# Re-interleaving all steps of a fused attention and highway kernel, with six short runs of dummy matmuls added

## The chip, the cores and the metric

The kernel runs on one core of a Trainium2 chip. The metric is the device time of one execution in microseconds (us). Eight executions of the kernel before were timed; their median is what the changed kernel is compared with. A traced execution adds, for every instruction of every engine, when it started and how long it was busy. The engines are TensorE (PE in the profile, with PEld for its weight loads), VectorE (DVE), ScalarE (ACT), GpSimd (POOL) and SyncE (SP), which here only issues DMAs.

## What is computed

`q`, `k`, `v` have shape 8 x 8 x 576 x 64 (batch, head, sequence, head size). An efficient attention is followed by a highway layer on 4608 tokens of width 512:

```python
q_s = softmax(q, over the 64 of a head)
k_s = softmax(k, over the 576 of the sequence)
kv  = einsum('bhsd,bhse->bhde', k_s, v)
x   = einsum('bhsd,bhde->bhse', q_s, kv)      # then (b, s) x (h, e): 4608 x 512
H   = max(x @ w_h, 0)
T   = sigmoid(x @ w_t + b_t)
out = T * H + (1 - T) * x
```

Inputs and output are float32; the matmuls run in float16.

## The kernel before, in words

The work is cut into batches b = 0 to 7, and into 37 kinds of step. Each kind is a small function, and one list, `order`, written out in the source, calls some 550 of them one after the other. Every engine executes its own share of that list strictly in the list's order, so the list decides all the queues; semaphores between engines are derived from the buffers.

For a batch, the steps are these.

- `load(b, "q" | "k" | "v")` issues one DMA of 1152 KB on SP's queue (two of 576 KB where a third argument 2 is given); `load_weight` brings `w_t` (one DMA of 1024 KB) and `w_h` (four of 256 KB). Each of the four input pools has three buffers; the weights pass through the same buffers as q and k. In the built program every DMA also waits until the DMA issued eight before it has completed.
- `exp_half` (ACT, L174) takes the exponential of half the heads of q or k. `cast_v` and `cast_v_head` bring v to float16 (POOL L185 and L193, ACT L191).
- `kv_half` (PE, 36 small matmuls, tile `psk`) forms k-transposed times v and, with a column of ones, the sums of k; `kv_norm` (DVE L212, L213) divides.
- `q_sums` or `q_sums_tree` (DVE L224, or L235 to L237), `q_recip` (DVE L242), then `q_scale_p` on POOL (L254; batch 0 has `q_scale_v` on DVE) normalise q. `q_trans` (PE, tile `pq`) and `q_copy` (DVE L274) transpose it; for batches 6 and 7 `q_turn` does that with two DMA transposes (L283, tile `qsD`) instead.
- `x_pair` and `x_left` (PE, tiles `px`, `px_l`) form x transposed; `x_copy` (ACT or DVE), `x_left_copy` and `x9_done` take it out of PSUM.
- The highway layer works in chunks c = 0 to 7, one per batch, and 8 and 9, which hold what 512 columns leave of each batch. For each chunk and each of four output blocks there is a `gate` (four matmuls, tile `pt`) with `tanh` on ACT (L392), a `carry` (four matmuls, tile `ph`) with `diff` on DVE (L405), and then `blend` on DVE (L413) and for some blocks `add_x` on POOL (L424). Here one `gate` or one `carry` of a chunk 0 to 7 is called a unit; there are 64.
- `out_tile` and `tile9` turn the result round on PE (tile `nat`), `out_copy` (L464) and `tile9_copy` copy it to a staging buffer and every fourth copy issues a 1 MB store. `last9` is the last of all.

The weights have steps of their own: `less_one` (POOL L122) subtracts the identity from `w_h`, and `cast_weight` casts one quarter of a matrix to float16, on POOL or DVE (L117) or ACT (L115). `gate_bias` turns the bias round on PE.

`warm_up(n)` issues n matmuls of a constant 128 x 512 operand whose result nobody reads, and `warm_mid(n, i, home)` does the same into a bank of its own. The kernel before issues 46 such dummies: 42 of them ahead of the first `q_trans`, two after `kv_norm(0)` in the list, two ahead of the first gate.

PSUM has four banks in the pool `ht`, two in `q2` and one each in `q1` and `nat`; a gate or a carry holds an `ht` bank from its first matmul until `blend` or `diff` has read it.

Of the kernel before, what the change touches and what calls it, by code (L numbers as in the profile page):

```python
# [18 lines left out]
def kernel(  # L19
# [12 lines left out]
    P = 128  # L32
# [422 lines left out]
    nat, nat2 = {}, {}  # L455
# [36 lines left out]
    def last9():  # L492
# [19 lines left out]
        ("warm_up", 24), ("load", 0, "q", 2), ("exp_half", 0, "q", 0), ("load", 1, "q"),  # L512
        ("load", 0, "v", 2), ("cast_v", 0, 1), ("warm_up", 6), ("exp_half", 0, "q", 1),
        ("warm_up", 1), ("q_sums", 0, 1), ("load", 0, "k", 2), ("warm_up", 4),
        ("warm_up", 2), ("load_bias",), ("cast_v", 0, 0), ("q_sums", 0, 0),
        ("load_weight", "t", "q32"), ("q_recip", 0), ("warm_mid", 5),
        ("q_scale_v", 0, 4, 9), ("q_trans", 0, 1, "q2"), ("exp_half", 1, "q", 0),
        ("load_weight", "h", "k32", 4), ("q_scale_v", 0, 0, 4), ("q_copy", 0, 1),
        ("load", 1, "k"), ("exp_half", 1, "q", 1), ("cast_weight", "t", 3, "P"),
        ("exp_half", 0, "k", 0), ("less_one", 1), ("q_trans", 0, 2, "nat"),  # L520
        ("q_sums_tree", 1, 0), ("q_sums_tree", 1, 1), ("q_trans", 0, 0),
        ("exp_half", 0, "k", 1), ("load", 1, "v", 2), ("kv_half", 0, 0), ("q_recip", 1),
        ("q_copy", 0, 2), ("kv_half", 0, 1), ("cast_weight", "t", 1, "P"), ("q_copy", 0, 0),
        ("kv_norm", 0), ("warm_up", 2), ("load", 2, "q"), ("less_one", 2),
        ("x_pair", 0, 0, False), ("cast_weight", "t", 0, "V"), ("less_one", 0),
        ("x_pair", 0, 1, False, ("ht", "ht")), ("x_copy", 0, 0, "AA"),
        ("x_copy", 0, 1, "AV"), ("gate_bias",), ("x_left", 0),
        ("cast_weight", "h", 1, "A", 0.5), ("less_one", 3), ("cast_weight", "t", 2, "V"),
        ("warm_up", 2), ("cast_weight", "h", 2, "A", 0.5),
        ("cast_weight", "h", 3, "A", 0.5), ("cast_weight", "h", 0, "A", 0.5),  # L530
        ("x_left_copy", 0), ("q_scale_p", 1, 4, 8), ("gate", 0, 2, "q2"), ("gate", 0, 0),
        ("gate", 0, 3, "nat"), ("tanh", 0, 2), ("exp_half", 1, "k", 1), ("carry", 0, 2),
        ("load", 2, "v", 2), ("q_trans", 1, 1), ("carry", 0, 1), ("diff", 0, 2),
        ("q_scale_p", 1, 0, 4), ("q_copy", 1, 1), ("tanh", 0, 0),
        ("cast_v_head", 1, 2, "P"), ("cast_v_head", 1, 1, "P"), ("exp_half", 1, "k", 0),
        ("cast_v_head", 1, 3, "A"), ("carry", 0, 0), ("blend", 0, 2), ("q_trans", 1, 0),
        ("gate", 0, 1), ("cast_v_head", 1, 0, "A"), ("kv_half", 1, 1), ("load", 2, "k"),
        ("diff", 0, 1), ("diff", 0, 0), ("tanh", 0, 1), ("q_copy", 1, 0), ("kv_half", 1, 0),
        ("blend", 0, 0), ("kv_norm", 1), ("q_scale_p", 1, 8, 9), ("q_trans", 1, 2),
        ("x_pair", 1, 0, False, ("ht", "ht")), ("tanh", 0, 3), ("exp_half", 2, "q", 0),  # L540
        ("q_copy", 1, 2), ("blend", 0, 1), ("x_pair", 1, 1, False, ("ht", "q2")),
        ("cast_v_head", 2, 2, "P"), ("x_copy", 1, 0, "AV"), ("x_copy", 1, 1, "AV"),
        ("gate", 1, 1), ("exp_half", 2, "q", 1), ("add_x", 0, 0), ("carry", 1, 2),
        ("cast_v_head", 2, 3, "A"), ("tanh", 1, 1), ("load", 3, "q"), ("q_sums_tree", 2, 0),
        ("cast_v_head", 2, 0, "P"), ("q_sums_tree", 2, 1), ("carry", 1, 1), ("diff", 1, 1),
        ("x_left", 1), ("carry", 0, 3), ("load", 3, "v"), ("gate", 1, 0),
        ("cast_v_head", 2, 1, "A"), ("q_recip", 2), ("exp_half", 2, "k", 1), ("tanh", 1, 0),
        ("load", 3, "k"), ("diff", 0, 3), ("blend", 1, 1), ("q_scale_p", 2, 0, 4),
        ("x_left_copy", 1), ("q_scale_p", 2, 8, 9), ("carry", 1, 0), ("q_scale_p", 2, 4, 8),
        ("diff", 1, 2), ("exp_half", 2, "k", 0), ("q_trans", 2, 0, "q1"),  # L550
        ("exp_half", 3, "q", 0), ("exp_half", 3, "q", 1), ("kv_half", 2, 1), ("diff", 1, 0),
        ("q_copy", 2, 0), ("load", 4, "q"), ("kv_half", 2, 0), ("gate", 1, 2),
        ("cast_v", 3, 1), ("blend", 0, 3), ("q_trans", 2, 1, "q1"), ("kv_norm", 2, 0, 1),
        ("blend", 1, 0), ("q_copy", 2, 1), ("carry", 1, 3),
        ("x_pair", 2, 0, False, ("nat", "q1")), ("add_x", 1, 1), ("kv_norm", 2, 1, 2),
        ("tanh", 1, 2), ("load", 4, "k"), ("q_trans", 2, 2, "q2"), ("load", 5, "q"),
        ("blend", 1, 2), ("x_copy", 2, 0, "AA"), ("q_sums", 3, 0), ("diff", 1, 3),
        ("gate", 1, 3), ("load", 4, "v"), ("x_pair", 2, 1, False, ("nat", "q1")),
        ("tanh", 1, 3), ("x_copy", 2, 1, "AV"), ("gate", 2, 1), ("cast_v", 3, 0),
        ("q_sums", 3, 1), ("carry", 2, 0), ("q_copy", 2, 2), ("exp_half", 3, "k", 1),  # L560
        ("q_recip", 3), ("gate", 2, 2), ("exp_half", 3, "k", 0), ("exp_half", 4, "q", 0),
        ("add_x", 1, 0), ("add_x", 0, 1), ("x_left", 2), ("blend", 1, 3),
        ("out_tile", 0, 1), ("q_scale_p", 3, 0, 4), ("exp_half", 4, "q", 1),
        ("x_left_copy", 2), ("diff", 2, 0), ("q_sums", 4, 0), ("carry", 2, 3),
        ("kv_half", 3, 0), ("diff", 2, 3), ("out_copy", 0, 1, "A"), ("exp_half", 4, "k", 1),
        ("kv_half", 3, 1), ("tanh", 2, 1), ("load", 5, "k"), ("q_scale_p", 3, 4, 9),
        ("q_trans", 3, 0, "q1"), ("carry", 2, 1), ("out_tile", 0, 0), ("q_copy", 3, 0),
        ("q_trans", 3, 1, "q1"), ("kv_norm", 3), ("out_copy", 0, 0, "A"),
        ("q_trans", 3, 2, "q2"), ("load", 6, "q"), ("diff", 2, 1), ("tanh", 2, 2),
        ("gate", 2, 0), ("exp_half", 5, "q", 1), ("q_copy", 3, 2), ("q_copy", 3, 1),  # L570
        ("q_sums", 4, 1), ("q_recip", 4), ("x_pair", 3, 0, True), ("out_tile", 0, 2),
        ("carry", 2, 2), ("x_copy", 3, 0, "A"), ("x_pair", 3, 1, True),
        ("out_copy", 0, 2, "A"), ("out_tile", 0, 3), ("q_scale_p", 4, 0, 4),
        ("blend", 2, 1), ("diff", 2, 2), ("x9_done", 3), ("tanh", 2, 0), ("blend", 2, 0),
        ("load", 5, "v"), ("gate", 2, 3), ("q_trans", 4, 0, "q1"), ("blend", 2, 2),
        ("q_sums", 5, 1), ("x_copy", 3, 1, "A"), ("q_copy", 4, 0), ("q_scale_p", 4, 4, 9),
        ("load", 7, "v"), ("carry", 3, 1), ("gate", 3, 0), ("load", 7, "q"),
        ("exp_half", 5, "q", 0), ("cast_v", 4, 0), ("carry", 3, 0), ("out_copy", 0, 3, "A"),
        ("tanh", 2, 3), ("q_trans", 4, 1, "q1"), ("out_tile", 0, 4), ("cast_v", 4, 1),
        ("diff", 3, 1), ("exp_half", 4, "k", 0), ("carry", 3, 3), ("diff", 3, 0),  # L580
        ("out_copy", 0, 4, "A"), ("out_tile", 0, 5), ("q_copy", 4, 1),
        ("q_trans", 4, 2, "q1"), ("kv_half", 4, 0), ("q_sums", 5, 0), ("tanh", 3, 0),
        ("add_x", 2, 0), ("kv_half", 4, 1), ("q_copy", 4, 2), ("q_recip", 5),
# [105 lines left out]
```

## Time and profile before

| what | value |
|---|---|
| median of 8 executions | 127.03 us (126.52 to 127.65) |
| the profiled execution's own time | 127.47 us |
| its span, first to last instruction | 125.7 us |
| mean granted TensorE clock | 0.972 |
| busy: PE, PEld | 111.1 us, 60.9 us |
| busy: DVE, ACT, POOL | 94.6 us, 92.7 us, 78.7 us |
| DMA | 41.24 MB, mean 328 GB/s |
| read from HBM, written to it | 30.41 MB, 9.44 MB |

The page cuts the span into 40 slices of 3.14 us and gives each engine's busy share in tenths; the row PEclk is the clock that TensorE was granted, in tenths of full speed. Matmuls overlap in their pipeline, so PE busy is not PE at its peak. The chain of waits follows the work back from the last instruction. "Idle before" is what an engine waited for. Times of stretches can be asked for with the busy time of every engine and the clock.

### The profile page before, as it was taken

The page shows a single profiled execution, that of the slowest core. Times are in us where ns is not written, and L with a number is a line of the kernel's source. Part 1 is how long each engine was busy: PE and PEld are TensorE (multiplying, and loading weights), DVE is VectorE, ACT ScalarE, POOL GpSimd, SP SyncE. Part 2 cuts the span into 40 slices and gives each one's busy share as a digit, 9 for nine tenths or more (in the row PEclk, how much of TensorE's full clock was granted, in tenths as well). Part 3 has the DMA queues.
Part 4 walks back from the last instruction along what each step waited for, and adds up shares of the span by engine and source line. Part 5 has one row for each costly group of instructions (what it writes and reads, how often), then busy time and mean ns, then how long its engine had stood idle before and what let it go on. Part 6 is the DMA issues. An engine that isn't in the chain of part 4 may idle for free.

```text
span 125.7 us, 3329 instructions
## 1 busy us (share of the span) xinstructions
PE 111.1 (88%) x1359; PEld 60.9 (48%) x1359; DVE 94.6 (75%) x179; ACT 92.7 (74%) x130; POOL 78.7 (63%) x75
## 2 busy tenths in 40 slices
PE   4999637999597898999999999999998999999950
PEld 1344412345342632644574564555464545599840
DVE  1077696019999999999999999689774736799960
ACT  4427436892995969989969969999993966866760
POOL 2000712974355995935988999999999424864610
PEclk9999996579999999999999999999999999999999
DMA  3999999999999999999999999994782702409984
GB/s 114 351 364 403 408 408 403 412 411 411 414 405 411 413 398 411 411 410 405 412 406 417 414 410 412 416 245 91 284 192 50 334 0 125 209 5 415 409 347 169
DMA packets 20583, 41.24 MB, mean 328 GB/s; under 512 B 5460, under 2 KB 5976, under 8 KB 19544
## 3 DMA queue, kind: packets, MB, share of 16 engines
q1 hardware_dynamic: 20568, 41.03, 85.9%
q8 instruction: 10, 0.16, 0.5%
q14 instruction: 5, 0.04, 0.1%
HBM read 30.41 MB, written 9.44 MB: 317 GB/s over the span
## 4 chain that ended last, share of the span: by engine, by line
PE 35%; DMA 23%; DVE 18%; POOL 11%; issue 4%; ACT 4%; SPq 3%; DVEq 1%; POOLq 0%; ACTq 0%
PE pt L64 14%; PE ph L64 11%; DMA v<-in_v_dram 9%; DMA k<-in_k_dram 9%; POOL eq L254 8%; PE nat L64 4%; DVE dd L405 4%; DMA qsD<-eq 4%; DVE r L224 3%; SPq L94 3%; DVE g L413 2%; PE pq L69 2%; DVE qsT L274 2%; POOL v L185 1%; DVE xT L361 1%
## 5 line engine op out<-in xcount | busy, mean ns | idle before, releaser
L64 PE MATMUL pt<-xT,w16t 128*128 128x512 f16 x128 | 34.6, 401 | 1.9 <-DVE xT L361 1.0
L254 POOL TENSOR_TENSOR eq<-eq,r 128x1024 f16<-128x1024 f16 (+2 forms) x16 | 29.7, 1877 | 8.7 <-DVE r L242 7.7
L64 PE MATMUL ph<-xT,w16h 128*128 128x512 f16 x128 | 32.1, 379 | 0.0
L405 DVE SCALAR_TENSOR_TENSOR dd<-xT,ph 128x512 f16<-128x512 f16 x32 | 21.3, 680 | 12.8 <-PE ph L64 12.5
L424 POOL TENSOR_TENSOR g<-g,xT 128x512 f16<-128x512 f16 x23 | 26.1, 1155 | 6.4 <-DVE g L413 6.4
L392 ACT ACTIVATE pt<-pt,bt 128x512 f32<-128x512 f32 (+1 forms) x40 | 24.6, 627 | 6.2 <-PE pt L64 5.5
L413 DVE SCALAR_TENSOR_TENSOR g<-pt,dd 128x512 f16<-128x512 f32 (+1 forms) x40 | 24.5, 626 | 4.1 <-ACT pt L392 3.3
L174 ACT ACTIVATE eq<-q 128x1152 f16<-128x1152 f32 x16 | 18.4, 1168 | 6.6 <-DMA q<-in_q_dram 5.5
L64 PEld LDWEIGHTS <-w16t 128*128 128x128 f16 x160 | 15.1, 101 | 16.1 <-issue 5.1
L464 ACT COPY o<-nat 128x512 f32<-128x512 f32 x28 | 16.7, 599 | 7.5 <-PE nat L64 6.4
L185 POOL CAST v<-v 128x1152 f16<-128x1152 f32 x12 | 13.6, 1148 | 11.3 <-DMA v<-in_v_dram 11.3
L64 PEld LDWEIGHTS <-w16h 128*128 128x128 f16 x160 | 14.6, 98 | 12.4 <-issue 1.0
L174 ACT ACTIVATE ek<-k 128x1152 f16<-128x1152 f32 x16 | 18.8, 1182 | 2.4 <-DMA k<-in_k_dram 2.4
L224 DVE TENSOR_REDUCE r<-eq 128x18 f32<-128x1152 f16 x12 | 16.0, 1344 | 5.3 <-ACT eq L174 5.3
L64 PE MATMUL nat<-ident,g 128*128 128x128 f16 x142 | 14.6, 220 | 0.0
L64 PEld LDWEIGHTS <-g 128*128 128x128 f16 x144 | 11.3, 98 | 5.4 <-DVE g L413 0.9
L64 PE MATMUL warm<-wide,ident 128*128 128x512 f16 x41 | 11.9, 452 | 1.8 <-DVE wide L144 1.8
L274 DVE COPY qsT<-pq 128x1024 f16<-128x1024 f16 (+1 forms) x18 | 9.7, 547 | 1.8 <-PE pq L69 1.6
L357 ACT CAST xT<-px 128x1024 f16<-128x1024 f32 x10 | 10.2, 1025 | 0.5 <-PE px L64 0.5
L69 PE MATMUL pq<-ident,eq 128*128 128x128 f16 x108 | 8.6, 220 | 0.9 <-POOL eq L254 0.7
L64 PEld LDWEIGHTS <-ident 128*128 128x128 f16 x46 | 4.8, 109 | 8.2 <-issue 3.1
L69 PEld LDWEIGHTS <-eq 128*128 128x128 f16 x108 | 6.6, 98 | 4.3 <-POOL eq L254 2.5
(53 smaller groups left out, 101.6 us busy)
## 6 DMA issues: line engine op xcount, KB each, us to landing
out_dram<-o SPq DMA_DIRECT2D x8, 1024.0 KB, 4.5
q<-in_q_dram SPq DMA_DIRECT2D x7, 1152.0 KB, 14.4
k<-in_k_dram SPq DMA_DIRECT2D x7, 1152.0 KB, 14.4
v<-in_v_dram SPq DMA_DIRECT2D x5, 1152.0 KB, 14.5
v<-in_v_dram SPq DMA_DIRECT2D x6, 576.0 KB, 10.7
q<-in_q_dram SPq DMA_DIRECT2D x2, 576.0 KB, 4.2
k<-in_k_dram SPq DMA_DIRECT2D x2, 576.0 KB, 11.2
w32t<-in_moe_w_t_dram SPq DMA_DIRECT2D x1, 1024.0 KB, 12.5
```

Of the source, the lines that this page charges most:

```text
L64: mm = lambda o, l, r, st, sp: nc.tensor.matmul(o, l, r, start=st, stop=sp, skip_group_check=True)
L69: nc.tensor.matmul(o, i, ident, is_transpose=True, start=True, stop=True, skip_group_check=True,)
L174: nc.scalar.activation(dst[b][:, :, 2 * a : 2 * a + 2, :], in32[which][b][:, 2 * a : 2 * a + 2].rearrange("p c n d -> p n c d"), AF.Exp,)
L185: nc.gpsimd.tensor_copy(o, i)
L224: nc.vector.reduce_sum(qsum[b][:, :, h], eq[b][:, :, h, :], axis=AX.X)
L254: nc.gpsimd.tensor_mul(e, e, r.broadcast_to(list(e.shape)))
L274: nc.vector.tensor_copy(qsT[b][:, :, n0:n1, :], turned_q.pop((b, g)))
L392: nc.scalar.activation(ps, ps, AF.Tanh, bias=bt2[:, ob : ob + 1], scale=0.5)
L405: nc.vector.scalar_tensor_tensor(dd, xv(ob), -0.5, ps, op0=ALU.mult, op1=ALU.max)
L413: nc.vector.scalar_tensor_tensor(gv(ob), th, 1.0, dd, op0=ALU.add, op1=ALU.mult)
L424: eng.tensor_add(gv(ob), gv(ob), xv(ob))
L464: copy(rows_of_four((g, n // 4))[:, n % 4, :], nat.pop((g, n)))
```

## The change

Only the list `order` is changed; all functions are the same. It has the same real steps as before. Their order differs almost everywhere, on every engine. What can be told apart:

- The DMAs at the start go q0, k0, bias, q1, v0, w_h, w_t instead of q0, q1, v0, k0, bias, w_t, w_h; from batch 3 on q4 is ahead of v3 and k3, and v7 is issued after the two transposes of batch 6.
- Steps on the weights of `w_h` come ahead of those on `w_t`.
- `warm_mid(2, i, "ht")` appears six times (i = 10, 16, 11, 1, 7, 18); together with the existing runs, now placed differently, there are 58 dummies, 31 of them ahead of the first `q_trans` and 23 between it and the first gate.
- The two transposes of batch 7 change places.

The list up to chunk 2's first matmuls, and the places further down that the text below speaks of:

```diff
-        ("warm_up", 24), ("load", 0, "q", 2), ("exp_half", 0, "q", 0), ("load", 1, "q"),
-        ("load", 0, "v", 2), ("cast_v", 0, 1), ("warm_up", 6), ("exp_half", 0, "q", 1),
-        ("warm_up", 1), ("q_sums", 0, 1), ("load", 0, "k", 2), ("warm_up", 4),
-        ("warm_up", 2), ("load_bias",), ("cast_v", 0, 0), ("q_sums", 0, 0),
-        ("load_weight", "t", "q32"), ("q_recip", 0), ("warm_mid", 5),
-        ("q_scale_v", 0, 4, 9), ("q_trans", 0, 1, "q2"), ("exp_half", 1, "q", 0),
-        ("load_weight", "h", "k32", 4), ("q_scale_v", 0, 0, 4), ("q_copy", 0, 1),
-        ("load", 1, "k"), ("exp_half", 1, "q", 1), ("cast_weight", "t", 3, "P"),
-        ("exp_half", 0, "k", 0), ("less_one", 1), ("q_trans", 0, 2, "nat"),
-        ("q_sums_tree", 1, 0), ("q_sums_tree", 1, 1), ("q_trans", 0, 0),
-        ("exp_half", 0, "k", 1), ("load", 1, "v", 2), ("kv_half", 0, 0), ("q_recip", 1),
-        ("q_copy", 0, 2), ("kv_half", 0, 1), ("cast_weight", "t", 1, "P"), ("q_copy", 0, 0),
-        ("kv_norm", 0), ("warm_up", 2), ("load", 2, "q"), ("less_one", 2),
-        ("x_pair", 0, 0, False), ("cast_weight", "t", 0, "V"), ("less_one", 0),
-        ("x_pair", 0, 1, False, ("ht", "ht")), ("x_copy", 0, 0, "AA"),
-        ("x_copy", 0, 1, "AV"), ("gate_bias",), ("x_left", 0),
-        ("cast_weight", "h", 1, "A", 0.5), ("less_one", 3), ("cast_weight", "t", 2, "V"),
-        ("warm_up", 2), ("cast_weight", "h", 2, "A", 0.5),
-        ("cast_weight", "h", 3, "A", 0.5), ("cast_weight", "h", 0, "A", 0.5),
-        ("x_left_copy", 0), ("q_scale_p", 1, 4, 8), ("gate", 0, 2, "q2"), ("gate", 0, 0),
-        ("gate", 0, 3, "nat"), ("tanh", 0, 2), ("exp_half", 1, "k", 1), ("carry", 0, 2),
-        ("load", 2, "v", 2), ("q_trans", 1, 1), ("carry", 0, 1), ("diff", 0, 2),
-        ("q_scale_p", 1, 0, 4), ("q_copy", 1, 1), ("tanh", 0, 0),
-        ("cast_v_head", 1, 2, "P"), ("cast_v_head", 1, 1, "P"), ("exp_half", 1, "k", 0),
-        ("cast_v_head", 1, 3, "A"), ("carry", 0, 0), ("blend", 0, 2), ("q_trans", 1, 0),
-        ("gate", 0, 1), ("cast_v_head", 1, 0, "A"), ("kv_half", 1, 1), ("load", 2, "k"),
-        ("diff", 0, 1), ("diff", 0, 0), ("tanh", 0, 1), ("q_copy", 1, 0), ("kv_half", 1, 0),
-        ("blend", 0, 0), ("kv_norm", 1), ("q_scale_p", 1, 8, 9), ("q_trans", 1, 2),
-        ("x_pair", 1, 0, False, ("ht", "ht")), ("tanh", 0, 3), ("exp_half", 2, "q", 0),
-        ("q_copy", 1, 2), ("blend", 0, 1), ("x_pair", 1, 1, False, ("ht", "q2")),
-        ("cast_v_head", 2, 2, "P"), ("x_copy", 1, 0, "AV"), ("x_copy", 1, 1, "AV"),
-        ("gate", 1, 1), ("exp_half", 2, "q", 1), ("add_x", 0, 0), ("carry", 1, 2),
-        ("cast_v_head", 2, 3, "A"), ("tanh", 1, 1), ("load", 3, "q"), ("q_sums_tree", 2, 0),
-        ("cast_v_head", 2, 0, "P"), ("q_sums_tree", 2, 1), ("carry", 1, 1), ("diff", 1, 1),
-        ("x_left", 1), ("carry", 0, 3), ("load", 3, "v"), ("gate", 1, 0),
-        ("cast_v_head", 2, 1, "A"), ("q_recip", 2), ("exp_half", 2, "k", 1), ("tanh", 1, 0),
-        ("load", 3, "k"), ("diff", 0, 3), ("blend", 1, 1), ("q_scale_p", 2, 0, 4),
-        ("x_left_copy", 1), ("q_scale_p", 2, 8, 9), ("carry", 1, 0), ("q_scale_p", 2, 4, 8),
-        ("diff", 1, 2), ("exp_half", 2, "k", 0), ("q_trans", 2, 0, "q1"),
-        ("exp_half", 3, "q", 0), ("exp_half", 3, "q", 1), ("kv_half", 2, 1), ("diff", 1, 0),
-        ("q_copy", 2, 0), ("load", 4, "q"), ("kv_half", 2, 0), ("gate", 1, 2),
-        ("cast_v", 3, 1), ("blend", 0, 3), ("q_trans", 2, 1, "q1"), ("kv_norm", 2, 0, 1),
-        ("blend", 1, 0), ("q_copy", 2, 1), ("carry", 1, 3),
-        ("x_pair", 2, 0, False, ("nat", "q1")), ("add_x", 1, 1), ("kv_norm", 2, 1, 2),
...
-        ("load", 7, "v"), ("carry", 3, 1), ("gate", 3, 0), ("load", 7, "q"),
...
-        ("carry", 5, 3), ("q_turn", 6, 4, 9), ("x9_done", 5), ("exp_half", 6, "k", 1),
...
-        ("q_turn", 6, 0, 4), ("q_scale_p", 7, 0, 4), ("tanh", 5, 2), ("kv_norm", 6),
...
-        ("tanh", 5, 1), ("q_scale_p", 7, 4, 9), ("q_turn", 7, 0, 4), ("out_tile", 1, 4),
...
-        ("out_copy", 1, 4, "A"), ("q_turn", 7, 4, 9), ("x9_done", 6), ("add_x", 5, 2),
...
-        ("tile9", 0, 4), ("add_x", 9, 0), ("tile9_copy", 0, 4, "A"),
-        ("tile9_copy", 1, 4, "V"), ("carry", 9, 3), ("blend", 9, 2), ("gate", 9, 3),
-        ("tile9", 3, 3), ("tanh", 9, 3), ("diff", 9, 3), ("tile9", 2, 3),
-        ("tile9_copy", 2, 3, "A"), ("tile9_copy", 3, 3, "V"), ("blend", 9, 3), ("last9",),
+        ("load", 0, "q", 2), ("warm_mid", 2, 10, "ht"), ("load", 0, "k", 2),
+        ("exp_half", 0, "q", 1), ("load_bias",), ("warm_up", 24), ("load", 1, "q"),
+        ("load", 0, "v", 2), ("cast_v", 0, 0), ("load_weight", "h", "k32", 4),
+        ("cast_v", 0, 1), ("load_weight", "t", "q32"), ("exp_half", 0, "q", 0),
+        ("q_sums", 0, 1), ("q_sums", 0, 0), ("exp_half", 0, "k", 0),
+        ("exp_half", 0, "k", 1), ("exp_half", 1, "q", 0), ("warm_mid", 5), ("q_recip", 0),
+        ("q_scale_v", 0, 4, 9), ("q_trans", 0, 1, "q2"), ("q_scale_v", 0, 0, 4),
+        ("gate_bias",), ("q_copy", 0, 1), ("warm_up", 6), ("warm_up", 1), ("q_trans", 0, 0),
+        ("warm_up", 4), ("exp_half", 1, "q", 1), ("q_sums_tree", 1, 0), ("less_one", 0),
+        ("kv_half", 0, 0), ("q_sums_tree", 1, 1), ("warm_up", 2), ("q_recip", 1),
+        ("warm_mid", 2, 16, "ht"), ("less_one", 1), ("q_trans", 0, 2, "nat"),
+        ("kv_half", 0, 1), ("warm_mid", 2, 11, "ht"), ("load", 1, "k"), ("less_one", 2),
+        ("q_copy", 0, 0), ("load", 1, "v", 2), ("load", 2, "q"), ("q_scale_p", 1, 4, 8),
+        ("cast_weight", "h", 0, "A", 0.5), ("warm_mid", 2, 1, "ht"), ("kv_norm", 0),
+        ("cast_weight", "h", 2, "A", 0.5), ("x_pair", 0, 0, False), ("less_one", 3),
+        ("cast_weight", "t", 1, "P"), ("q_copy", 0, 2), ("cast_weight", "h", 1, "A", 0.5),
+        ("x_pair", 0, 1, False, ("ht", "ht")), ("x_copy", 0, 1, "AV"),
+        ("x_copy", 0, 0, "AA"), ("x_left", 0), ("cast_weight", "h", 3, "A", 0.5),
+        ("x_left_copy", 0), ("warm_up", 2), ("q_trans", 1, 1), ("cast_weight", "t", 3, "P"),
+        ("warm_up", 2), ("q_scale_p", 1, 0, 4), ("cast_weight", "t", 0, "V"),
+        ("cast_weight", "t", 2, "V"), ("gate", 0, 0), ("q_copy", 1, 1),
+        ("gate", 0, 2, "q2"), ("carry", 0, 2), ("q_trans", 1, 0), ("diff", 0, 2),
+        ("tanh", 0, 0), ("carry", 0, 0), ("cast_v_head", 1, 1, "P"), ("carry", 0, 1),
+        ("tanh", 0, 2), ("q_copy", 1, 0), ("cast_v_head", 1, 2, "P"), ("load", 2, "v", 2),
+        ("exp_half", 1, "k", 0), ("blend", 0, 2), ("exp_half", 1, "k", 1),
+        ("cast_v_head", 1, 0, "A"), ("gate", 0, 1), ("load", 2, "k"), ("diff", 0, 0),
+        ("kv_half", 1, 0), ("diff", 0, 1), ("cast_v_head", 1, 3, "A"),
+        ("q_scale_p", 1, 8, 9), ("tanh", 0, 1), ("cast_v_head", 2, 2, "P"),
+        ("exp_half", 2, "q", 0), ("blend", 0, 0), ("kv_half", 1, 1),
+        ("exp_half", 2, "q", 1), ("kv_norm", 1), ("q_trans", 1, 2),
+        ("x_pair", 1, 0, False, ("ht", "ht")), ("x_pair", 1, 1, False, ("ht", "q2")),
+        ("blend", 0, 1), ("x_copy", 1, 0, "AV"), ("x_copy", 1, 1, "AV"), ("carry", 0, 3),
+        ("q_copy", 1, 2), ("cast_v_head", 2, 0, "P"), ("load", 3, "q"),
+        ("gate", 0, 3, "nat"), ("tanh", 0, 3), ("x_left", 1), ("q_sums_tree", 2, 0),
+        ("cast_v_head", 2, 3, "A"), ("q_sums_tree", 2, 1), ("x_left_copy", 1),
+        ("q_recip", 2), ("q_scale_p", 2, 0, 4), ("gate", 1, 1), ("tanh", 1, 1),
+        ("carry", 1, 2), ("carry", 1, 1), ("exp_half", 2, "k", 0), ("diff", 0, 3),
+        ("diff", 1, 2), ("diff", 1, 1), ("blend", 0, 3), ("carry", 1, 0), ("blend", 1, 1),
+        ("diff", 1, 0), ("load", 4, "q"), ("gate", 1, 0), ("q_scale_p", 2, 4, 8),
+        ("cast_v_head", 2, 1, "A"), ("q_trans", 2, 0, "q1"), ("kv_half", 2, 0),
+        ("q_copy", 2, 0), ("exp_half", 2, "k", 1), ("gate", 1, 2), ("kv_norm", 2, 0, 1),
+        ("tanh", 1, 0), ("q_trans", 2, 1, "q1"), ("exp_half", 3, "q", 1), ("load", 3, "v"),
+        ("tanh", 1, 2), ("add_x", 0, 1), ("blend", 1, 0), ("q_scale_p", 2, 8, 9),
+        ("kv_half", 2, 1), ("q_copy", 2, 1), ("add_x", 1, 0), ("add_x", 1, 1),
+        ("kv_norm", 2, 1, 2), ("add_x", 0, 0), ("q_sums", 3, 1), ("gate", 1, 3),
+        ("exp_half", 3, "q", 0), ("q_sums", 3, 0), ("x_pair", 2, 0, False, ("nat", "q1")),
+        ("warm_mid", 2, 7, "ht"), ("load", 3, "k"), ("x_copy", 2, 0, "AA"),
...
+        ("gate", 4, 3), ("diff", 4, 2), ("q_turn", 6, 0, 4), ("out_tile", 1, 1),
+        ("x_copy", 5, 1, "A"), ("tanh", 4, 3), ("blend", 4, 2), ("add_x", 4, 0),
+        ("gate", 5, 2), ("q_turn", 6, 4, 9), ("carry", 5, 0), ("kv_half", 6, 1),
+        ("load", 7, "v"), ("out_copy", 1, 1, "A"), ("blend", 4, 1), ("add_x", 4, 2),
...
+        ("tanh", 5, 0), ("q_scale_p", 7, 0, 4), ("out_copy", 1, 3, "A"),
...
+        ("out_copy", 1, 5, "A"), ("blend", 5, 0), ("add_x", 5, 0), ("q_scale_p", 7, 4, 9),
+        ("carry", 5, 2), ("tanh", 5, 1), ("cast_v", 7, 1), ("x_pair", 6, 1, True),
+        ("cast_v", 7, 0), ("diff", 5, 1), ("diff", 5, 2), ("x_copy", 6, 1, "A"),
+        ("carry", 5, 3), ("q_turn", 7, 4, 9), ("out_tile", 1, 4), ("blend", 5, 2),
...
+        ("q_turn", 7, 0, 4), ("exp_half", 7, "k", 1), ("gate", 5, 3), ("carry", 6, 1),
...
+        ("carry", 9, 2), ("tile9", 1, 4), ("blend", 9, 1), ("tile9_copy", 0, 4, "A"),
+        ("gate", 9, 2), ("tanh", 9, 2), ("blend", 9, 0), ("gate", 9, 3), ("diff", 9, 2),
+        ("tile9_copy", 1, 4, "V"), ("blend", 9, 2), ("add_x", 9, 1), ("tanh", 9, 3),
+        ("blend", 9, 3), ("add_x", 9, 0), ("tile9", 3, 3), ("tile9", 2, 3),
+        ("tile9_copy", 2, 3, "A"), ("tile9_copy", 3, 3, "V"), ("last9",),
+        ("warm_mid", 2, 18, "ht"),
```

## The prediction

> **What bounds the kernel now.** I read the page's rows by slices first, then the chain of waits, then busy time by stretches of the first 27 us, then each engine's timeline there. The page:
>
> ```profile
> PE   4999637999597898999999999999998999999950
> DVE  1077696019999999999999999689774736799960
> POOL 2000712974355995935988999999999424864610
> PEclk9999996579999999999999999999999999999999
> DMA  3999999999999999999999999994782702409984
> ```
>
> From slice 15 (47 us) to slice 37, PE is nearly solid; DMA is full until 82 us, DVE from 28 us on. PE's holes and the only fall of the clock lie in the first third. So I add up PE's real work with the chain's prices where PE carries it: a unit 0.86 us (64: 55.3), the same for chunks 8 and 9 0.44 (16: 7.0), a batch's `kv_half` pair 0.73 (5.8), its three `q_trans` 1.01 (6.1), its x steps 0.80 (6.4), an `out_tile` 0.22 to 0.34 (9.0), `tile9` and `last9` 1.3. Sum: 90.9 us. From the first real matmul (12.98) to the last (121.7) pass 108.7, so 17.8 are lost. At `x_pair(1, 0)`, at 32.76, seven units, two kv pairs, six `q_trans` and one batch's x steps are done (10.3 us) in 19.8: 9.5 of the 17.8 go there, 8.3 in the next 89 us.
>
> Stretches of 3.4 us around that loss (columns: length, then busy of PE, PEld, DVE, ACT, POOL, the granted clock, DMA share, GB/s):
>
> ```profile
> 9.60:13.00 3.40, 3.40 (x18) 1.50 (x17) 2.28 (x6) 2.22 (x2) 0.25 (x1) 1.00 1.03 405
> 13.00:16.40 3.40, 1.63 (x55) 1.34 (x53) 2.70 (x5) 1.97 (x2) 1.99 (x2) 1.00 1.04 408
> 16.40:19.80 3.40, 1.74 (x49) 0.78 (x50) 2.84 (x10) 0.62 (x2) 0.62 (x1) 0.99 1.05 405
> 19.80:23.20 3.40, 2.91 (x15) 1.06 (x15) 1.47 (x5) 2.56 (x5) 2.05 (x5) 0.50 1.04 408
> 23.20:26.60 3.40, 3.40 (x10) 1.22 (x8) 0.00 (x0) 3.28 (x6) 3.40 (x3) 0.50 1.04 411
> ```
>
> Two half-empty stretches, then 6.8 us at half clock. The chain and the waits:
>
> ```profile
> 3.89 11.68 DMA k<-in_k_dram
> ...
> 16.01 11.74 DMA v<-in_v_dram
> 27.75 0.02 issue
> 27.77 1.26 ACT v L191 x2
> ...
> 39.10 4.34 POOL eq L254 x3
> ```
>
> ```profile
> DVE dd L405 <- PE ph L64: 12.5, 9, 6.6
> ```
>
> v1 lands at 27.75. DVE idles 6.6 us, until 27.87, for its first `diff`: in the list the `w_h` casts end after 24 us, and the carries behind them run slowly. From then DVE is full.
>
> **Dummies.** 31 instead of 42 lie ahead of the first `q_trans`. Warm ones follow each other in 0.216 us, so 11 fewer let PE go 2.4 us earlier; `q_trans(0, 1)` can run when its scale ends (11.2), at 11.2 instead of 12.98. That is worth nothing by itself: `kv_half(0)` still waits for data. Loads land in the order of issue about 1 us after the summed GB/s row has covered their bytes (v0, 3.54 MB, summed to 11.75 us, cast at 12.75). k0 and v0 swap, so the later of the two lands where k0 did, 14.16 and 15.6 us for the halves, and POOL's cast (1.15) takes the place of ACT's exponential (1.16): kv at 15.4 and 16.8, as before. `kv_norm(0)` comes at 18.1 to 19.2 against 18.39, whether or not DVE's sums run as slowly beside POOL (1.06 against 0.45 us for one addition). Between there and the first gate lie 23 dummies, 5.0 us, placed in waits: cover 15.7 to 21.5; without it 5.0. The pair of `warm_mid(2, 7)`, at about 41 us, costs 0 to 0.43; I take 0.43. The last pair is behind `last9`, beside the final store: 0.
>
> **The first gate.** Before, `w_t` quarter 3 is cast at 21.52 to 22.13 and the gate runs from there. After, `w_t` is last of the weights; POOL's wait for `w_h` before ended at 21.15, so this position lands at 21.2 to 22.0. Two casts on DVE (0.42 each) and two on POOL (0.61 each) end at 22.4 to 23.2: 0.3 to 1.1 later, I take 0.7. POOL's `q_scale_p(1, 4, 8)`, 1.9 us, now goes ahead of `less_one(3)`, but ends before `w_t` lands.
>
> **The clock.** On the same grid I place 2.9 us of PE work in 13.0 to 16.4 (1.63 before) and 2.0 to 2.5 in 16.4 to 19.8 (1.74). The page TensorE: Matmul & The Clock Gate of the Trainium skill (section "Why this matters for your kernels") speaks against a gain: it asks only that no gap exceed about 3 us. The longest gap here was 1.25 us, yet the clock fell; the rows decide. By the rule neither order should fall, filling is worth 0 and the sum is 126.5; by the rows the sum of busy time counts and the fall goes. Saved: real gate work from 22.1 to 26.6 at half speed, 4.5/2 = 2.2 us. With it, by v1's landing PE has done six units instead of four.
>
> **Batch 1.** v1 lands at the same bytes. Its heads take two casts on POOL and two on ACT (0.67 each), ending 28.4 to 29.1; kv 0.37, `kv_norm` 0.6: `x_pair(1, 0)` at 29.8 against 32.76, 3.0 earlier with one unit less (0.86). **PE leads by 2.1.** DVE, fed with carries from about 24.8, has its seven 0.6 us steps done by 29 and leads by 3.0.
>
> **Batch 2.** ACT does `exp_half(2, q)` (q2 lands near 30) ahead of the two x copies, so `gate(1, 1)` ends near 33.5 against 34.98, one unit ahead: lead 2.35. `q_recip(2)` comes at 35.1 against 38.96 and POOL's chain piece at 39.10 starts at 35.2. `x_pair(2, 0)` at 41.0 against 44.90 with equal units: 3.9, less 0.43 for the dummies: 3.5.
>
> **Batches 3 to 7.** At later `x_pair`s the units done are 22, 28, 37, 45, 53 against 22, 29, 37, 46, 52: the shape stays, so the lead lasts if POOL and SP let it. POOL: from 35.2 to the end of `q_scale_p(6)` it has 39.0 us of work (1.88 and 2.31 per scale, 1.13 per `add_x`, 1.12 per cast); its waits for DVE's reciprocals, walked through with 1.26 per sum and 0.6 per step, are 3.5 (5.8 before): 77.7, or 80.0 with the old waits, against 83.5. Then 11.0 us of casts, adds and scales to the end of `q_scale_p(7)` (8.7 before): 88.7 to 91.0. Both transposes of batch 7 are now behind it; one took 4.98, the other's issue adds 0.2 to 1.35: `x_pair(7, 0)` at 93.9 to 97.3, middle 95.5, against 97.15, with one unit and one `out_tile` more done (1.14). Lead 1.0 to 4.4, middle 2.8. q4 ahead of k3 and the later k5: DMA stays full, nothing waited on k after 16 us, and earlier issues put k3's landing near 46 where kv(3) wants it near 48: 0, up to 1.0 if it slips. v7 is a rival, below.
>
> **The tail.** From the last gate's end (120.12) the last copy ended 2.14 later. After: tanh 0.65, blend 0.41, `last9` 0.2, copy 0.4 and the tiles between: 2.0. Zero.
>
> **Sum.** Between 2.1 and 3.5, with 2.8 from POOL's side: 2.8 off the span of 125.7, or off that execution's 127.47: 124.7. It was 0.44 above the median 127.03; against the median, **124.2 us**.
>
> **Rivals.**
>
> - *The clock falls all the same.* For: the second stretch gets only 2.0 to 2.5, and no row shows the limit. Against: 1.63 alone did not do it, and the two together rise from 3.4 to about 5. Price 2.2: 126.4, or up to 126.8.
> - *The lead is given back.* In-order engines stall elsewhere: k3, or POOL on DVE's reciprocals. For: DVE and POOL are full from 28 and 58 us. Against: both start earlier themselves. All 2.8 back: 127.0.
> - *v7 late: slower.* Its load moves from ahead of the k6 load to behind both transposes of batch 6 on SP's queue, which wait for `q_scale_p(6, 4, 9)`. Issue at 80 to 82; `cast_v(7)` (2.24), the kv pair, `kv_norm` and `x_pair(7, 0)` wait behind it, and all of PE after that. POOL asks for v7 after `q_scale_p(7)`, so 9.4 us to landing cost nothing. Stores landed in 4.5 us in an emptier queue, and DMA is then nearly idle; v loads took 9.0 to 15.9 when it was full. At 15.9: landing 97.5, casts 99.8, kv and norm 101.1; x 5.6 after the middle: 129.8. At the median 13.8: 127.7. It turns slower than before from a landing of about 95.
> - *More than walked:* if POOL's waits shrink to nothing, 122.8.
>
> **Chances.** Forecast 0.57 (its own range 123.0 to 125.6), clock 0.12, given back 0.12, v7 0.13, more 0.06. A measurement of this kernel can tell 0.5% (0.6 us) from no change. Faster by more: 0.57 + 0.06 + part of the clock's case and of the lead partly given back = 0.70; within: 0.16; slower: 0.14. The range 122.7 to 127.1 leaves out most of the v7 case and bits of the others.
>
> **What the changed profile would show.** Right: clock 1.00 in all slices (mean 0.99 or more); first `diff` at 24 to 25.5 us; `x_pair(1)` at 29 to 30.5; third POOL scale near 35; `x_pair(2)` near 41; `x_pair(7)` at 94 to 97; a span near 122.9. Wrong: 0.5 in PEclk after 19 us; waits of POOL `v` or PE `psk` on the DMA of v late in the span; a wait on `qsD` of more than 2 us; PE idle of over 2 us in all between 45 and 95 us.

## The result, and the profile after

The changed kernel takes 125.11 us (median of 11 executions, 124.32 to 125.51) against 126.9 for the kernel before on the same chips (32 executions, 125.96 to 127.65): ratio 0.9856, 95% interval 0.9831 to 0.988. It is 1.8 us faster; 2.8 were forecast. Times are medians, while ratios and intervals compare only executions within 1.5% of their kernel's fastest; after's profiled execution, 126.58 us (span 124.5, clock 0.985), lies above all eleven others (clocks 0.991 to 1.000) and is in neither. So where its head matters a second trace stands beside it: that of `c1_k5` below, which issues three loads at 49.9 to 58.1 us instead of 60.7 to 63.5 and takes the same time.

The rows of the page of after, to be read against those of before:

```profile
PE   4995894999988998999999979998999999999970
...
PEclk9999999599999999999999999999999999999999
```

One slice of PEclk stands below 9 instead of three, and PE's early holes are shallower. The stretches of after (columns as in the prediction):

```profile
13.00:16.40 3.40, 2.73 (x54) 1.59 (x53) 2.11 (x4) 2.22 (x2) 1.63 (x2) 1.00 1.05 409
16.40:19.80 3.40, 2.27 (x46) 1.04 (x44) 3.26 (x8) 1.78 (x3) 3.03 (x5) 1.00 1.06 411
19.80:23.20 3.40, 2.86 (x29) 1.60 (x30) 2.84 (x8) 2.09 (x4) 2.93 (x4) 0.80 1.03 404
23.20:26.60 3.40, 3.40 (x12) 1.34 (x11) 0.22 (x1) 1.17 (x2) 2.63 (x3) 0.70 1.04 409
```

and those of `c1_k5`:

```profile
13.00:16.40 3.40, 3.06 (x55) 1.77 (x54) 2.37 (x5) 1.99 (x2) 1.90 (x2) 1.00 1.05 408
16.40:19.80 3.40, 2.18 (x49) 1.05 (x51) 3.25 (x8) 1.78 (x3) 3.03 (x5) 1.00 1.06 403
19.80:23.20 3.40, 2.90 (x31) 1.27 (x23) 2.79 (x6) 2.09 (x4) 2.81 (x5) 1.00 1.03 404
23.20:26.60 3.40, 3.40 (x22) 1.83 (x23) 1.23 (x3) 2.72 (x4) 2.48 (x2) 1.00 1.04 411
```

With 2.73 + 2.27 us of work in the two thin stretches the clock still fell, for 3.4 us instead of 6.8; with 3.06 + 2.18 it did not. The wait of DVE's `diff` for the carries, which stood at 12.5 us in all, 6.6 at most, in before, is now, in after:

```profile
DVE dd L405 <- PE ph L64: 8.3, 6, 3.6
```

One thing is new in after's chain of waits, as start and duration:

```profile
79.49 7.49 DMA qsD<-eq
```

That is the second DMA transpose of batch 6; in the chain of before only batch 7's appeared, with 4.98.

What the traces have in common is seen in the starts of the first `px` matmul of `x_pair(b, 0)`, read from each PE timeline (us):

| kernel | b = 1 | b = 6 | b = 7 | span |
|---|---|---|---|---|
| before | 32.76 | 88.19 | 97.17 | 125.7 |
| after, profiled | 31.37 | 87.04 | 97.17 | 124.5 |
| `c1_k5` | 29.83 | 85.17 | 95.30 | 123.3 |
| `a1_no_six` | 30.47 | 86.02 | 96.15 | 123.6 |
| `a2_no_dummies` | 33.40 | 88.83 | 98.96 | 126.7 |
| `e_v7` | 29.12 | 87.42 | 99.12 | 127.1 |
| `d2_k7` | 29.69 | 83.95 | 94.49 | 122.1 |

A delay at b = 1 is passed on almost whole: from b = 1 to b = 6 lie 55.3 to 55.7 us in the first five rows, that of before included. The head decides, and the two last rows show what else can.

### The profile page after: what moved, and what is told of

Read it like the earlier page. It is cut to its first block, busy times and chain, and to the rows that moved or that the text cites. A ratio compares the mean times of both kernels' runs of the same rounds, so it can differ in the third digit from the quotient of the medians.

```text
span 124.5 us, 3361 instructions
## 1 busy us (share of the span) xinstructions
PE 111.8 (90%) x1371; PEld 61.9 (50%) x1371; DVE 96.3 (77%) x179; ACT 93.1 (75%) x130; POOL 79.6 (64%) x75
## 4 chain that ended last, share of the span: by engine, by line
PE 35%; DVE 23%; DMA 14%; POOL 13%; issue 5%; ACT 4%; SPq 2%; ACTq 0%; POOLq 0%; DVEq 0%
PE ph L64 12%; PE pt L64 12%; DMA q<-in_q_dram 8%; POOL eq L254 7%; DMA qsD<-eq 6%; PE nat L64 6%; POOL g L424 4%; DVE dd L405 4%; DVE g L413 4%; DVE r L224 3%; DVE qsT L274 2%; DVE t L235 2%; DVE t L236 2%; DVE xT L361 2%; PE px L64 2%
## 5 line engine op out<-in xcount | busy, mean ns | idle before, releaser
L64 PE MATMUL pt<-xT,w16t 128*128 128x512 f16 x128 | 33.6, 390 | 0.0
L185 POOL CAST v<-v 128x1152 f16<-128x1152 f32 x12 | 13.6, 1152 | 13.3 <-DMA v<-in_v_dram 13.3
L174 ACT ACTIVATE ek<-k 128x1152 f16<-128x1152 f32 x16 | 18.3, 1163 | 2.0 <-DMA k<-in_k_dram 2.0
L64 PE MATMUL warm<-wide,ident 128*128 128x512 f16 x53 | 14.9, 422 | 1.8 <-DVE wide L144 1.8
L69 PE MATMUL pq<-ident,eq 128*128 128x128 f16 x108 | 9.2, 222 | 1.8 <-ACT ek L174 1.3
L69 PEld LDWEIGHTS <-eq 128*128 128x128 f16 x108 | 7.2, 98 | 5.9 <-ACT ek L174 1.7
L64 PEld LDWEIGHTS <-ident 128*128 128x128 f16 x58 | 5.6, 105 | 7.9 <-issue 2.5
## 6 DMA issues: line engine op xcount, KB each, us to landing
k<-in_k_dram SPq DMA_DIRECT2D x7, 1152.0 KB, 13.3
```

What stands on the lines that cost most here:

```text
L64: mm = lambda o, l, r, st, sp: nc.tensor.matmul(o, l, r, start=st, stop=sp, skip_group_check=True)
L69: nc.tensor.matmul(o, i, ident, is_transpose=True, start=True, stop=True, skip_group_check=True,)
L174: nc.scalar.activation(dst[b][:, :, 2 * a : 2 * a + 2, :], in32[which][b][:, 2 * a : 2 * a + 2].rearrange("p c n d -> p n c d"), AF.Exp,)
L185: nc.gpsimd.tensor_copy(o, i)
```

## Experiments

Every kernel was timed beside the kernel before (medians of before 126.72 to 126.85).

**Dummies or order?** First after without the six short runs (46 dummies left, as many as before has):

```diff
-("warm_mid", 2, 10, "ht"),
-("warm_mid", 2, 16, "ht"),
-("warm_mid", 2, 11, "ht"),
-("warm_mid", 2, 1, "ht"),
-("warm_mid", 2, 7, "ht"),
-("warm_mid", 2, 18, "ht"),
```

> The changed kernel without its six short runs of dummies (12 of 58); all else as it is. If the gain rests on the clock being held by dummies, the fall lasts longer: mean granted clock 0.972 to 0.987 instead of about 0.993, 126.0 to 127.0 us. If the gain rests on the new order of the real steps: 125.1 within 0.4, or up to 0.4 less because the pair at 43.6 us goes.

125.59 us, ratio 0.9922 (0.9887 to 0.9957), clocks mostly 0.97 to 0.985: between the two forecasts. So the order with the old number of dummies brings 1.1 us, and the six runs 0.5 more. That order includes where the 46 dummies stand, though: 17 of them come after `q_trans(0, 1)`, against 4 in before.

Then after with none of the 27 dummies behind `q_trans(0, 1)`:

```diff
 ("q_trans", 0, 1, "q2"),
...
-("warm_up", 6), ("warm_up", 1),
-("warm_up", 4),
-("warm_up", 2),
-("warm_mid", 2, 16, "ht"),
...
-("warm_mid", 2, 18, "ht"),
```

> The changed kernel with only the 31 dummies ahead of the first transposes; the other 27 are out. By the clock: the fall is as long as in the kernel before (6.8 us) or longer, 126.6 to 127.5 us. By the order of the real steps: at most 125.4 us, whatever the clock does.

127.81 us, ratio 1.0024 (0.9981 to 1.0068): no gain is left. That is near the forecast by the clock and far from the one by the order. Its stretches:

```profile
13.00:16.40 3.40, 0.91 (x38) 0.70 (x37) 2.35 (x4) 2.00 (x2) 1.94 (x2) 0.82 1.05 407
16.40:19.80 3.40, 1.03 (x42) 0.89 (x44) 3.21 (x8) 1.78 (x3) 3.03 (x5) 0.50 1.05 390
19.80:23.20 3.40, 2.49 (x26) 1.43 (x18) 2.45 (x5) 2.09 (x4) 3.40 (x5) 0.50 1.04 405
23.20:26.60 3.40, 2.58 (x7) 0.86 (x7) 1.72 (x2) 0.66 (x1) 1.50 (x2) 0.50 1.04 411
26.60:30.00 3.40, 3.40 (x18) 1.59 (x17) 1.06 (x2) 2.80 (x4) 1.24 (x2) 0.67 1.04 411
```

Half clock from before 16.4 to almost 29 us: 13.7 us of it (each row's loss of clock, 2.01 in all, times 2 times 3.4).

And the reverse, before with 13 dummies put into its own waits of 14 to 21 us:

```diff
 ("q_trans", 0, 0),
+("warm_up", 4),
...
 ("kv_half", 0, 0),
+("warm_up", 3),
...
-("kv_norm", 0), ("warm_up", 2),
+("kv_norm", 0), ("warm_up", 6),
...
 ("x_left", 0),
+("warm_up", 2),
```

> The kernel before with 13 more dummies put in the waits that its trace shows between 14 and 21 us; no real step moved. By the clock: clock 0.985 or more, 124.7 to 125.7 us, most of the gain. By the order of the real steps: 126.4 to 127.2 us even where the clock is held, because v of batch 1 lands at 27.7 us anyway.

125.16 us, ratio 0.9877 (0.9832 to 0.9922): 1.6 us from thirteen dummies, without any new order; the clocks of its other executions are 0.989 to 1.000. In its one trace (127.69 us, the longest of its executions) `x_pair(1)` comes at 30.32, but PE then waits 1.9 us on `qsD` at 87.8 and the clock falls there instead, so how its usual execution uses the lead isn't shown.

**Which half of the order?** Each hybrid follows one list up to `x_pair(1, 1)` and then takes all that is left in the other's order.

```diff
 ("x_pair", 1, 0, False, ("ht", "ht")), ("x_pair", 1, 1, False, ("ht", "q2")),
-("blend", 0, 1), ("x_copy", 1, 0, "AV"), ("x_copy", 1, 1, "AV"), ("carry", 0, 3),
+("gate", 0, 3, "nat"), ("tanh", 0, 3), ("q_copy", 1, 2), ("blend", 0, 1),
...
```

> The changed list up to and with the second x pair of batch 1, and from there the steps that remain in the order of the kernel before. If the gain is made in the first 30 us and the rest only passes it on: 124.6 to 125.5 us. If the later re-interleaving carries a share: 125.8 to 126.8. If the later part of the change costs something (the load of k of batch 5 behind the first store, 0.75 us; the transposes): 124.0 to 124.6.

Head of after, tail of before: 125.88 us, ratio 0.9941 (0.9914 to 0.9968).

```diff
 ("q_copy", 1, 2), ("blend", 0, 1), ("x_pair", 1, 1, False, ("ht", "q2")),
-("cast_v_head", 2, 2, "P"), ("x_copy", 1, 0, "AV"), ("x_copy", 1, 1, "AV"),
+("cast_v_head", 2, 2, "P"), ("exp_half", 2, "q", 1), ("x_copy", 1, 0, "AV"),
...
```

> The list of the kernel before up to and with the second x pair of batch 1, and from there the steps that remain in the order of the changed one. If the gain is made in the first 30 us: 126.7 to 127.5 us. If the later part carries a share: 125.3 to 126.3.

Head of before, tail of after: 126.9 us, ratio 1.0016 (0.9989 to 1.0042). The new tail gives nothing by itself. The new head gives 0.8, less than was forecast if the head made the whole gain, but its trace shows that the join itself costs something (a line of ACT's timeline, then one of PE's):

```profile
33.35 1.07 ACT L361 CAST xT<-px 128x512 f16<-128x512 f32 x2
33.98 1.08 PE L64 MATMUL pt<-xT,w16t 128*128 128x512 f16 x4 [1.93 <-DVE t L235]
```

PE waits 1.93 us for the copy of x that this gate reads. (The bracket names whatever finished last; DVE's part of the copy had ended at 32.40, and ACT's first cast, 0.59 us long, ends at 33.94.) ACT makes its part only after both exponentials of q2 and a `tanh`. Neither list has this order: the head of after puts the exponentials ahead of the copy, the tail of before puts this gate right behind it. From `x_pair(1)` to `x_pair(2)` the hybrid takes 13.3 us (30.46 to 43.75), before 12.1 and `b1_dummies` 12.0; from `x_pair(2)` to `x_pair(6)` it takes 43.29, exactly as before does. So the old tail passes the rest of the lead on, and about 1.2 us are lost where the two lists meet. Without that loss the head would be worth some 2.0 us, all of the gain; that is an estimate from these two numbers.

**k5.** In after PE waits 0.75 us for `ek` at 72.49, since the load of k5 stands behind the first store.

```diff
 ("load", 6, "q"),
+("load", 5, "k"), ("load", 6, "k"), ("load", 7, "q"),
...
-("load", 5, "k"),
...
-("load", 6, "k"),
...
-("load", 7, "q"),
```

> The changed kernel with the loads of k of batch 5, k of 6 and q of 7 issued ahead of the first store instead of behind it; nothing else. The store waits for its copies from 50 to 60 us and holds them up, the transfer rate falls to 327 and 250 GB/s in two slices, and TensorE later waits 0.75 us for the exponential of k5. If that wait reaches the end: 124.2 to 124.8 us, and both slices at 400 GB/s. If it is made up elsewhere: 125.1 within 0.3.

125.21 us, ratio 0.9875 (0.9847 to 0.9903): the wait is gone and the time is after's. Something later takes it up. In this trace, that is at `x_pair(6)`:

```profile
85.16 0.22 PE L64 MATMUL px_l<-qsD,kvn 64*64 64x64 f16 x2 [1.04 <-DMA qsD<-eq]
```

**v7 early, and k7 late.** First the load of v7 put ahead of batch 6's transposes:

```diff
 ("load", 7, "k"),
+("load", 7, "v"),
...
 ("q_turn", 6, 4, 9), ("carry", 5, 0), ("kv_half", 6, 1),
-("load", 7, "v"),
```

> The changed kernel with v of batch 7 loaded ahead of the first store's successors and of the two transposes, as early as its buffer allows; nothing else. The rival of the prediction said that v7 would be late: then 0.3 to 1.5 us are gained. The trace shows its cast starting with no wait for the DMA, so: 125.1 within 0.3.

130.13 us, ratio 1.0252 (1.0217 to 1.0287): 5 us slower than after, which nothing in the expectation allowed for. SP's queue in its trace (start, duration; an issue that takes long is an SP that is held):

```profile
66.88 2.80 SPq L94 DMA_DIRECT2D v<-in_v_dram  x1
73.28 0.36 SPq L467 DMA_DIRECT2D out_dram<-o  x1
73.74 10.35 SPq L283 DMA_TRANSPOSE qsD<-eq  x2
```

and PE and its stretches there:

```profile
87.40 0.22 PE L64 MATMUL px_l<-qsD,kvn 64*64 64x64 f16 x2 [3.33 <-DMA qsD<-eq]
```

```profile
83.40:86.80 3.40, 0.66 (x4) 0.20 (x2) 1.59 (x3) 0.42 (x1) 3.33 (x3) 1.00 1.15 146
86.80:90.20 3.40, 2.80 (x21) 1.18 (x22) 0.07 (x1) 2.07 (x3) 3.40 (x3) 0.67 0.80 322
```

Issuing the two transposes takes 10.35 us instead of 7.77 in `c1_k5`, with one load of 1152 KB more on the DMA ahead of them. They land late, PE stands for 3.33 us, and the clock falls after that: `x_pair(7)` comes 3.8 us later than in `c1_k5`. The load that was moved is one that nobody was waiting for.

So the opposite was tried: the load of k7, too, behind both transposes.

```diff
-("load", 7, "k"),
...
 ("q_turn", 6, 4, 9), ("carry", 5, 0), ("kv_half", 6, 1),
+("load", 7, "k"),
 ("load", 7, "v"),
```

> After, with the load of k7 issued behind both transposes of batch 6, directly ahead of the load of v7. Theory (the transposes queue behind loads on a full DMA): in the traces of after's order PE waits 0.6 to 1.2 us on qsD at x_pair(6), since the second transpose of batch 6 takes 7.3 to 7.6 us to land while DMA is full of loads. With 1.15 MB (2.8 us at 410 GB/s) fewer ahead of it it lands 1 to 2.8 us sooner, the wait on qsD goes and PE-bound work behind it moves: 0.6 to 1.2 us off after's 125.1, so 123.9 to 124.5, and DMA full until about 77 us. Rival (the transposes are slow by themselves, or PE has no other slack): 125.1, wait unchanged. Rival (k7 and v7 come late now): waits of ACT ek or POOL v on DMA near 88 us and a time over 125.6.

124.17 us, ratio 0.9805 (0.9763 to 0.9847): 0.9 less than after, and the fastest version here. Its queue and PE:

```profile
73.65 5.61 SPq L283 DMA_TRANSPOSE qsD<-eq  x2
79.31 0.57 SPq L94 DMA_DIRECT2D k<-in_k_dram  x1
```

```profile
83.93 0.22 PE L64 MATMUL px_l<-qsD,kvn 64*64 64x64 f16 x2
```

The last line, the one that had the 1.04 us in `c1_k5`, has no wait in brackets any more. In 76.4 to 79.8 us `c1_k5` moved 412 GB/s, `d2_k7` 232: there the loads were gone and the transposes had the DMA to themselves. ACT did not wait for k7, and POOL 0.7 us for v7: some of the 1.2 us won at `x_pair(6)` is lost again by `x_pair(7)`, which is 0.8 earlier than in `c1_k5`.

**More dummies.** Ten more in the waits that were left in 14 to 21 us:

```diff
+("warm_up", 3),
 ("kv_half", 0, 0),
...
 ("warm_mid", 2, 1, "ht"),
+("warm_up", 5),
...
-("warm_up", 2), ("q_trans", 1, 1),
+("warm_up", 4), ("q_trans", 1, 1),
```

> The changed kernel with 10 more dummies in the three waits left between 14.9 and 21.6 us. The profile of the changed kernel still had one stretch of 3.4 us at half clock (21.9 to 25.2). If holding the clock pays: clock 0.997 or more in most runs, 124.0 to 124.7 us, and a smaller spread. If what is left of the fall is hidden by the landing of v of batch 1: 125.1 within 0.3. If the dummies overrun their waits: 125.2 to 125.8.

127.12 us, ratio 1.0034 (1.0001 to 1.0066): 2 us slower than after, outside all three forecasts, with clocks (0.985 to 0.998) nearly as high. The trace offered a cause. From the groups of tile `w16t` (min/median/max in ns):

```profile
L117 DVE CAST w16t<-w32t x2: 674/1396/2119, 21.2 to 21.8; 128x512 f16<-128x512 f32 x2
```

One of DVE's two casts took 2.12 us, while POOL ran a `q_scale_p`; in after the two took 0.43 and 0.83, and the first gate did not wait for them. Test: one of the two casts on ACT.

```diff
-("cast_weight", "t", 2, "V"),
+("cast_weight", "t", 2, "A"),
```

> The version with ten more dummies, but with quarter 2 of w_t cast by ACT instead of DVE. Theory (collision): in the trace of the ten-dummy version one of DVE's two w_t casts took 2.12 us instead of 0.43, beside POOL's 1.9 us q_scale_p(1, 0, 4), and the gate waited 1.4 us on it; with one cast on ACT (0.66, ACT is idle there) DVE has one cast and the gate starts about 1 us earlier: about 1 to 1.4 us off its 127.12, so 125.7 to 126.1, first diff near 25.4, x_pair(1) near 29.9. Rival (the dummies themselves hold up PE's queue): the casts are incidental, 127.0 as before, with PE waits merely moved. Rival (the tail): the head's gain is taken back by the batch 6 transposes: x_pair(1) earlier but x_pair(6) still near 87.

126.8 us, ratio 1.0062 (1.0022 to 1.0101). The long cast is gone and `x_pair(1)` is back at 29.84 (30.86 with it), as the theory had it; the time isn't. The theory falls. The same edit on top of the late k7:

> Both edits on after: k7's load behind the transposes of batch 6, and quarter 2 of w_t cast by ACT. In after's profiled run the casts of POOL and DVE ran side by side in 1.2 us, so the second edit should give 0 to 0.4 there and only take away the runs in which DVE's cast falls beside POOL's scale. Theory: 123.6 to 124.4. If the gate is bound by w_t's landing (21.1 to 22.2 us) instead: the same as with k7 alone. If neither helps: 125.1.

124.83 us, ratio 0.9852 (0.9805 to 0.9899): no gain over k7 alone, and only 0.3 us less than after, although in this trace too PE no longer waits for `qsD`. So the gain of the late k7 is 0.9 us in one version and 0.3 in the other, from six executions each; its size isn't settled.

What `c3_more` and `d1_c3_act` share is at the very end. After, transfers from 117 us on (KB each, median us to landing):

```profile
out_dram<-o SPq DMA_DIRECT2D x1, 512.0 KB, 2.9
out_dram<-o SPq DMA_DIRECT2D x1, 384.0 KB, 2.5
out_dram<-o SPq DMA_DIRECT2D x1, 128.0 KB, 2.4
```

`c3_more`, the same (`d1_c3_act` has the same three times):

```profile
out_dram<-o SPq DMA_DIRECT2D x1, 512.0 KB, 4.4
out_dram<-o SPq DMA_DIRECT2D x1, 384.0 KB, 3.9
out_dram<-o SPq DMA_DIRECT2D x1, 128.0 KB, 3.7
```

Ten dummies are 20 instructions of PE (a weight load and a matmul each). With them q8, the queue for instructions, carries 11 packets of 16 KB instead of 10 (both versions, by their pages), and the eleventh runs beside the last stores. If it is the number that counts, ten dummies where they can hold up nobody must cost the same:

```diff
-("warm_up", 24),
+("warm_up", 29),
...
-("warm_mid", 2, 18, "ht"),
+("warm_mid", 7, 18, "ht"),
```

> After with ten more dummies where PE has nothing to do: five in front (PE idles 1.26 us ahead of the first q_trans; five take 1.08) and five behind last9, beside the final stores. As in the version with ten dummies in the waits, PE gets 20 instructions more. Theory (instruction fetch): the traces of the two ten-dummy versions show an eleventh packet of 16 KB on the instruction queue at 118 to 121 us, beside the last stores, which then land in 3.7 to 4.4 us instead of 2.4 to 2.9. The same number of instructions brings the same packet wherever the dummies stand: the last stores land 1.1 to 1.4 us later, 126.2 to 126.6 us. Rival (the dummies hurt only where they hold up PE's queue in 14 to 22 us): 125.1, ten packets. Rival (the stores were slow for another reason): eleven packets, yet stores in 2.5 us and 125.1.

126.88 us, ratio 1.0041 (1.0006 to 1.0076), clocks 0.991 to 1.000. Its page and its last transfers:

```profile
q8 instruction: 11, 0.18, 0.5%
```

```profile
GB/s 540 270 424 617 270 347 617 424 193 87 366 386 424 376 395 376 159 431 369 354 398 313 333 121 63 22 29 22 29 17 22 0 0 0 0 0 0 0 0 0
...
out_dram<-o SPq DMA_DIRECT2D x1, 512.0 KB, 4.7
out_dram<-o SPq DMA_DIRECT2D x1, 384.0 KB, 4.1
out_dram<-o SPq DMA_DIRECT2D x1, 128.0 KB, 3.9
```

The same packet and the same late stores, though these ten stand elsewhere. The row (slices of 0.21 us) shows how: for about 1.3 us only 17 to 29 GB/s flow, and a sixteenth of 410 is 25.6. That fits 15 of the 16 DMA engines being done while one, presumably that with the packet, still has its share of the stores to do; which engine it is, the trace doesn't tell. From `x_pair(7)` to the end of the span pass 28.9 us here, 27.4 in after and 28.0 in `c1_k5`, so the end costs 0.9 to 1.6 of the 1.8 us. Beside that, `x_pair(6)` comes 0.9 later than in `c1_k5` (86.05 against 85.17). A wait of 0.83 us for `ek` ahead of it, which `c1_k5` doesn't have, is part of that; the rest is not settled.

## Why the prediction was right or wrong

- **Right: the mechanism.** The gain comes from the head and the clock carries it: without dummies in the waits none is left, and dummies alone give 1.6 of the 1.8 us. PE busy in 13.0 to 19.8 us against the length of the fall makes a series: 1.94 us, 13.7 us of half clock (`a2_no_dummies`); 3.37, 6.9 (before); 4.24, 3.4 (`a1_no_six`); 5.00, 3.4 (after's profiled execution); 5.24, none in the head (`c1_k5`). The longest wait of PE in 13 to 24 us does not order them: 1.25 us in before, 2.27 in `a1_no_six`, 1.24 in after, 1.22 in `c1_k5`.
- **Not shown: where the limit lies.** The 3.41 us just ahead of after's fall (18.45 to 21.86) hold 1.75 us of PE's work, and 18.06 to 21.47 us in `c1_k5` hold 1.76, without a fall; 32.10 to 35.51 us in `h_after_head_1` hold 1.53, again without one. So after stands near an edge that PE busy alone does not fix. My "against", that one thin stretch alone did not do it, fails too: `a1_no_six`, with 3.12 and then 1.12, fell.
- **The rival "the clock falls all the same"** holds in one trace of after by half, and with it came a sign that I had named as wrong, 0.5 in PEclk after 19 us. It is the exception: a fall of 3.4 us takes 0.014 off the mean clock, and the other executions' clocks are 0.991 to 1.000.
- **Right: the first gate, batch 1 and batch 2.** Forecast and `c1_k5`: first `diff` 24 to 25.5, 25.44; `x_pair(1)` 29.8, 29.83; third POOL scale 35.2, 35.36; `x_pair(2)` 41.0, 41.31. In after's profiled execution all of these come 1.5 to 1.9 later.
- **Right: POOL, and v7.** End of `q_scale_p(6)` forecast at 77.7 to 80.0, measured 76.9 in `c1_k5`, a little earlier still, and 78.6 in after; `x_pair(7)` 95.5, measured 95.30. v7 was issued at 83.49 and POOL never waited for it; `e_v7` shows that the rival had the sign the wrong way round, since early is what costs here.
- **Incomplete: "the lead lasts if POOL and SP let it".** I priced the transposes of batch 7 and not those of batch 6. With the load of v7 behind them they were no longer last on SP's queue, but k7 was still ahead of them on the full DMA, and PE waits 0.6 to 1.0 us for them. With k7 behind them the wait is gone, for a gain of 0.9 us in `d2_k7` and 0.3 in `d3_k7_act`.
- **Wrong: the last step of the sum.** The span was forecast at 122.9; the median span of after's eleven executions is 122.8. That it fits so well is in part luck, since the wait for the transposes of batch 6 was not priced and POOL was faster than walked. The 0.9 us between 124.2 and 125.11 come from what I subtracted from. I took the 2.8 us found in one execution of before off the median of all. That execution's span, 125.7, is 0.8 above the median span of 29 others (124.9); against them the span shrinks by 2.1. Where the 0.8 us lie isn't shown: the clock of that execution, 0.972, is also the median of the 29, so a longer fall is not what sets it apart. A further 0.2 is what lies around the span: 1.79 for before, 1.95 after (medians).
- **Not weighed: the number of instructions.** The 12 added dummies were priced by where they stand. It happened to be enough: 1371 matmuls bring ten packets of instructions (1372 in `b1_dummies` too), 1381 bring eleven.

Open: a usual execution of `b1_dummies` was not traced. That it reaches 125.16 with before's tail, while the hybrid with that tail stays at 125.88, fits the 1.2 us that the hybrid loses at its join; where else the two differ isn't shown.

## What to carry to other kernels

Where the clock falls after half-empty stretches, try dummies in the existing waits before a new order: thirteen of them gave nearly all that this reordering gave. Count them, though: an added instruction has a place in the stream and a share in a packet that must be fetched. And where the DMA is full, as here until 80 us, look at what stands ahead of a transfer that PE will wait for: a load issued "in good time" that could have waited cost 5 us in `e_v7`. When two orders are joined to find which half counts, look at the join before reading the sum.

## What was not expected of the hardware

- The falls of the clock came as 3.4, 6.8 and about 13.7 us at exactly 0.50: multiples of some 3.4 us. Besides the wait of 3.33 us in `e_v7`, a wait of 1.9 us in `b1_dummies` was followed by one; a wait of 1.93 us in `h_after_head_1`, which ended at 33.98, was not.
- With one 16 KB packet of instructions beside them, the final stores landed after 3.7 to 4.7 us instead of 2.4 to 2.9.
- A DVE cast of 128x512 from float32 took 2.12 us instead of 0.43 while POOL multiplied float16 tiles; beside POOL's own casts it took 0.83.
